# The order of loads and work in a fused attention and FFN block on one core: FFN weights moved in the sync engine's queue

## The chip, the cores and the metric

The kernel runs on one core of a Trainium2 chip. The time is the device time of one execution in microseconds (us), the median of several runs. One further execution was profiled; its own time and its span, from the first to the last instruction, are given below. The engines are named as in the profile: PE (TensorE, matmuls) with its weight loads PEld, DVE (VectorE), ACT (ScalarE), POOL (GpSimd) and SP (SyncE, which here issues every DMA transfer).

## What is computed

A transformer block for 2048 tokens of width 512, all in bf16: a layernorm, linear attention with 32 heads of 16, a residual, a layernorm, an FFN of width 1792 with a ReLU, and a residual.

```python
def _A_ref(x, wqkv, wo):
    B, S, D = x.shape
    H = 32; Dh = D // H
    qkv = (lambda x, *d: x.transpose(*d))((x @ wqkv).reshape(B, S, 3, H, Dh), 2, 0, 3, 1, 4)
    q, k, v = qkv[0], qkv[1], qkv[2]
    phi = lambda t: jnp.where(t > 0, t + 1, jnp.exp(t)) + 1e-6
    pq, pk = phi(q), phi(k)
    kv = jnp.einsum("bhsd,bhse->bhde", pk, v)
    z = jnp.einsum("bhsd->bhd", pk)
    num = jnp.einsum("bhqd,bhde->bhqe", pq, kv)
    den = jnp.einsum("bhqd,bhd->bhq", pq, z)[..., None] + 1e-6
    o = num / den
    return (lambda x, *d: x.transpose(*d))(o, 0, 2, 1, 3).reshape(B, S, D) @ wo
...
h = x + _A_ref(_layernorm(x, axis=-1), A_wqkv, A_wo)
h2 = h + _B_ref(_layernorm(h, axis=-1), B_w1, B_w2)   # relu(x @ w1) @ w2
```

## The kernel before

The order of all work is written out by hand. The string `ORDER` holds 567 words; each word names a small function `op_...` and its numbers, and a loop at the end calls them one after the other. There is no scheduler behind it: each engine runs its instructions in the order of the words that fall to it, and each instruction waits on semaphores for what it reads and overwrites. So an order has five queues in it, and an instruction that waits holds up everything behind it on its engine. A DMA transfer's place in SP's queue is the place of its word.

The 2048 tokens are 16 tiles of 128 rows (the numbers 0 to 15 behind most words) and four blocks of 512 tokens (0 to 3). The words, by stage:

- Loads, by SP: `lx.t.n` loads n tiles of x; `lk`, `lq`, `lv`, `lo` load the weights of k, q, v and the output projection (`lv` and `lo` in halves of 256 KB), `l1.0.2` and `l1.2.2` the two halves of w1 and `l2.0.7` and `l2.7.7` those of w2, 896 KB each. All but `lx` go through the helper `load_d` (L216).
- First layernorm: `S` and `A` (statistics, DVE), `R` (rstd, ACT), `N` (normalize, DVE). The normalized tile is turned with PE (`T`, and `E` on ACT copies it out) for tiles 0 to 4, and by a DMA transpose `X` (L290, SP) for the others.
- `K.t.b` (L298) and `Q.c.j.b` (L306) are the projections into PSUM bank b; `F`, `U`, `M`, `D` and `qF`, `qU`, `qM`, `qD` make phi of them (exp and relu on ACT, min and add on DVE). `G.t` (L350) accumulates the product of the normalized x and phi(k) in banks 4 to 7. `za`, `zf`, `zhi`, `zlo`, `z`, `zc`, `zh` sum phi(k) over the tokens; `gA`, `gD`, `kv`, `kx`, `m`, `mA`, `mD` make the state times the projections of v and of the output, `m_sb`.
- The denominators, block by block: `d4.c` (L422, PE), `dl4.c` and `dx4.c` (ACT, logarithm and exponential) give the reciprocals. They have to stand on 16 partitions each, so `wb.c` (L450) stores them to a DRAM scratch and eight transfers `rb.c.0` to `rb.c.7` (L453, 64 KB each) read them back, each repeated over 16 partitions, into `rr`. `rr` is one buffer for all four blocks. `dm.c.jb.2` (L466, DVE, two for each block) multiplies phi(q) by `rr` into `pqs`.
- `h.t.b` (L475, PE) multiplies `pqs` with `m_sb`, and `hD.t` (L481, DVE) adds x. Second layernorm: `s`, `a` (DVE), `r` (ACT), `n` (DVE) or `nA` (ACT, L258), then a PE transpose `t` with `v` (DVE) or `e` (ACT), or a DMA transpose `x` (L291, SP).
- FFN: `p.c.f.b` (L490) and `ph` (half of the tokens, L499), with ReLU by `pA` (ACT, L505) or `pD` (DVE, L510); `f.t.b.f0.n` (L519) is the second product, seven matmuls a word, `fo` (L527, DVE) scales and adds h, `fd` (L534, SP) stores.

The middle of SP's queue before reads, in order: ten `X` from `X.6`, `lv.2.2 lv.0.2 lo.0.2 lo.2.2 wb.0 l1.0.2`, the eight rows `rb.0`, `l1.2.2 l2.0.7 wb.1 x.1 x.0 rb.1.2 l2.7.7`, the other seven rows `rb.1`, `wb.2`, the eight rows `rb.2`, `wb.3 x.7` and the eight rows `rb.3`. Transfers of one queue are spread over 16 DMA engines; one is complete when all sixteen shares have landed.

Of the kernel before, what the change touches and what calls it, by code (L numbers as in the profile page):

```python
# [15 lines left out]


ORDER = """
table const masks warm.70.7.64 warm.2.7 lx.0.1 S.0 A.0 R.0.1 lx.1.1 lx.2.2 S.1 N.0.0.2 T.0.4.0.2 A.1 lk.0.4 S.2
N.0.2.2 lx.4.2 A.2 R.1.1 N.1 S.3 T.0.0.2.2 A.3 E.0.0.2 R.2.1 lx.6.2 E.0.2.2 T.1.3 E.1 N.2 R.3.1 lq.0.4 K.0.1.0.2  # L20
K.0.1.2.2 S.5 T.2.2 N.3 K.1.6.0.2 S.4 F.0.1 K.1.6.2.2 T.3.5 E.2 A.5 M.0.1 lx.8.4 K.2.4.0.2 K.2.4.2.2 U.0.1 E.3
A.4 S.6 S.7 R.4.2 A.6 N.4 Q.0.0.3 K.3.7.0.2 A.7 F.1.1 U.2.1 lx.12.4 N.5 R.6.2 F.2.1 M.1.1 S.11 X.5 U.1.1 N.6
D.0.1 D.1.1 X.6 T.4.5 Q.0.3.1 K.3.7.2.2 A.11 E.4 M.2.1 N.7 S.9 D.2.1 X.7 F.3.1 A.9 Q.0.1.4 S.12 M.3.1 U.3.1
qU.0.0.2 qF.0.0.2 K.4.5 K.5.6 A.12 S.10 S.8 S.13 U.4.2 F.4.2 A.10 A.8 Q.0.2.0 A.13 qM.0.0.2 D.3.1 R.8.2 N.8
K.6.2 M.4.2 R.10.2 K.7.3 G.1 S.14 N.9 A.14 R.12.2 D.4.2 X.8 G.2 G.3 G.0 G.5 N.13 qF.0.2.2 X.9 U.6.2 F.6.2 S.15
qM.0.2.2 A.15 X.13 R.14.2 qU.0.2.2 N.12 K.8.2 K.9.3 qD.0.0.2 M.6.2 N.11 N.14 N.10 X.12 X.11 D.6.2 qD.0.2.2 X.10
X.14 F.8.2 G.4 K.13.1 U.8.2 za.4.1 K.12.0 M.8.2 G.7 K.11.3 K.10.2 G.6 N.15 F.12.2 D.8.2 za.6.0 U.12.2 M.12.2
K.14.0 za.8.0 X.15 F.10.2 U.10.2 M.10.2 K.15.1 zf D.10.2 zhi D.12.2 lv.2.2 F.14.2 M.14.2 G.9 G.8 zlo lv.0.2 G.10
Q.1.1.3 lo.0.2 U.14.2 D.14.2 z.2.2 z.3.2 z.1.2 z.0.2 zc zh G.14 d4.0.0 dl4.0 dx4.0 G.12 G.15 G.13 G.11 Q.1.0.2
lo.2.2 gA.0.2 qF.1.0.2 Q.1.2.0 gD.2.2 kv.1.5 kv.3.5 kv.0.5 kv.2.5 Q.1.3.1 qU.1.0.2 Q.2.0.4 qM.1.0.2 qF.1.2.2 kx  # L30
m.1.3 m.0.2 m.2.6 qU.1.2.2 m.3.7 Q.2.1.5 wb.0 l1.0.2 rb.0.4 rb.0.3 rb.0.7 mA.2.2 rb.0.5 rb.0.1 qU.2.0.2 qD.1.0.2
Q.2.2.0 Q.2.3.1 qM.1.2.2 mD.0.2 rb.0.2 rb.0.0 rb.0.6 qF.2.0.2 dm.0.0.2 dm.0.2.2 l1.2.2 h.1.6 qU.2.2.2 qD.1.2.2
d4.1.2 hD.1 s.1 a.1 h.0.4 hD.0 s.0 l2.0.7 dl4.1 dx4.1 a.0 n.0 Q.3.0.3 h.3.7 Q.3.1.4 hD.3 nA.1 qF.2.2.2 wb.1 s.3
h.2.1 a.3 x.1 Q.3.3.6 qU.3.0.2 hD.2 n.3 s.2 Q.3.2.5 a.2 t.3.7 n.2 qM.2.2.2 qF.3.0.2 x.0 ph.0.0.2.0 v.3
ph.0.2.0.0 t.2.4 qU.3.2.2 v.2 ph.0.3.1.0 qM.2.0.2 qM.3.0.2 ph.0.1.3.0 r.0.4 qF.3.2.2 ph.0.1.3.1 ph.0.0.2.1
ph.0.3.1.1 qM.3.2.2 qD.2.2.2 pA.0.0.2 p.0.9.5 p.0.8.4 pA.0.8.2 ph.0.2.0.1 qD.3.2.2 qD.2.0.2 qD.3.0.2 d4.2.2.2
rb.1.2 l2.7.7 rb.1.1 rb.1.3 rb.1.0 rb.1.7 p.0.6.6 p.0.7.7 rb.1.4 rb.1.5 rb.1.6 dm.1.2.2 dm.1.0.2 pD.0.2.2 dl4.2
h.7.5 dl4.3 dx4.2 wb.2 h.5.3 rb.2.4 pD.0.6.2 hD.7 h.6.0 hD.5 s.7 hD.6 a.7 s.5 s.6 p.0.5.6 p.0.4.5 a.5 rb.2.3
rb.2.5 pD.0.4.2 rb.2.6 a.6 p.0.12.1 h.4.3 p.0.11.7 hD.4 p.0.10.6 p.0.13.2 n.6 dx4.3 s.4 rb.2.0 rb.2.7 rb.2.1
rb.2.2 f.1.0.0.7 n.7 a.4 n.5 n.4 dm.2.0.2 dm.2.2.2 pD.0.12.2 pD.0.10.2 h.11.3 h.9.5 wb.3 x.7 rb.3.0 rb.3.6 h.8.2  # L40
h.10.1 r.4.4 hD.11 hD.9 s.11 hD.8 rb.3.3 rb.3.2 a.11 hD.10 s.9 f.1.0.7.7 rb.3.5 rb.3.7 rb.3.1 rb.3.4 s.8
dm.3.0.2 dm.3.2.2 s.10 f.3.4.0.7 f.2.7.0.7 a.9 a.8 h.12.6 a.10 fo.1 hD.12 h.13.1 h.14.3 n.9 n.11 s.12 hD.14
r.8.4 h.15.6 x.4 x.6 x.5 f.2.7.7.7 a.12 hD.13 hD.15 s.14 s.15 s.13 a.14 a.15 a.13 n.14 n.8 n.10 n.12 n.13 fo.2
fd.1 x.11 x.9 p.1.11.3 p.1.10.2 p.1.6.0 p.1.7.1 p.1.9.6 p.1.8.5 n.15 f.3.4.7.7 f.0.7.0.7 pA.1.6.2 pA.1.10.2
pD.1.8.2 x.10 fo.3 f.0.7.7.7 p.1.1.5 p.1.0.4 fo.0 p.1.5.1 p.1.4.0 r.12.4 x.8 p.1.12.2 p.1.3.7 fd.3 pA.1.0.2 x.13
fd.0 p.1.2.6 p.1.13.3 pA.1.4.2 pD.1.2.2 pA.1.12.2 p.2.10.0 p.2.11.1 pA.2.10.2 x.15 x.14 p.2.9.4 p.2.8.3 p.2.4.6
p.2.5.7 p.2.3.2 x.12 fd.2 p.2.2.1 pD.2.8.2 p.2.6.4 pA.2.4.2 p.2.7.5 pA.2.2.2 pD.2.6.2 p.2.13.2 p.2.12.1
pA.2.12.2 f.4.6.0.7 f.4.6.7.7 f.5.7.0.7 fo.4 f.5.7.7.7 fo.5 f.7.3.0.7 p.2.0.6 p.2.1.7 pA.2.0.2 f.7.3.7.7 fo.7
p.3.0.4 p.3.1.5 f.6.1.0.7 p.3.2.2 pD.3.0.2 p.3.3.3 pA.3.2.2 f.6.1.7.7 fo.6 p.3.7.7 p.3.6.6 p.3.13.3 p.3.12.2
pA.3.6.2 fd.5 p.3.9.5 pD.3.12.2 p.3.8.4 pA.3.8.2 p.3.10.1 p.3.11.2 pA.3.10.2 p.3.4.6 p.3.5.7 pD.3.4.2 f.8.2.0.7  # L50
fd.7 f.15.5.0.14.0.2 fo.15.0.2 fd.4 f.8.2.7.7 fo.8 f.9.3.0.7 f.9.3.7.7 fd.6 f.13.5.0.7 fd.15.0.2 f.13.5.7.7
f.11.1.0.7 fo.9 fd.9 f.11.1.7.7 fo.13 fo.11 fd.8 f.12.4.0.7 f.12.4.7.7 fo.12 fd.13 fd.11 fd.12 f.14.2.0.7
f.14.2.7.7 fo.14 fd.14 f.10.6.0.7 f.10.6.7.7 fo.10 fd.10 f.15.0.0.14.3.1 fo.15.3.1 fd.15.3.1 f.15.1.0.14.2.1
fo.15.2.1 fd.15.2.1
"""


# [1 line left out]
def kernel(  # L59
# [155 lines left out]
    def load_d(dst, src, k, n):
        nc.sync.dma_start(out=dst[:, k : k + n, :], in_=src[:, k : k + n, :])  # L216
# [353 lines left out]
```

## Time and profile before

| | us |
|---|---|
| median of 3 runs (lowest, highest) | 170.49 (169.94, 170.64) |
| the profiled execution | 170.41 |
| its span | 168.7 |
| PE busy | 163.0 (97%) |
| DVE busy | 98.4 (58%) |
| ACT busy | 64.1 (38%) |
| granted TensorE clock | 1.00 |

The profiled execution is one run: its time is the span and what lies around it. Engines and DMA over the span, in 40 slices of 4.2 us (tenths):

```profile
PE   7799999999999997999999999999999999999993
...
DVE  3999999932689958999999511212204122213213
ACT  3799976815898763010011422442020242000000
...
DMA  5974155714896591413621335000011000011111
```

The slices show PE full from the third to the last but one, apart from the sixteenth (63 to 67 us); DVE full from 4 to 34 us and for most of 42 to 88; ACT mostly idle from 67 us on; DMA busiest at 4 to 8, 42 to 51 and 59 to 63 us. Times in the text are microseconds from the span's start.

### The profile page before, as it was taken

How to read it: one execution, taken by the hardware profiler on the slowest of the kernel's cores; microseconds unless marked ns; L12 is line 12 of the kernel's file. 1: busy time of each engine (PE TensorE's matmuls, PEld its weight loads, DVE VectorE, ACT ScalarE, POOL GpSimd, SP SyncE). 2: the span in 40 equal slices, each digit the busy share in tenths (PEclk: the TensorE clock that was granted, in tenths of full speed). 3: DMA queues.
4: the chain of work that ended last, by engine and by line, in shares of the span. 5: the costliest groups of instructions: out<-in, count | busy, mean ns of one | idle time of the engine just before them, and what ended most of it. 6: DMA issues, size and time to landing. Idle time of an engine off the chain costs nothing.

```text
span 168.7 us, 2429 instructions
## 1 busy us (share of the span) xinstructions
PE 163.0 (97%) x924; PEld 79.3 (47%) x924; DVE 98.4 (58%) x204; ACT 64.1 (38%) x98; POOL 4.9 (3%) x21
## 2 busy tenths in 40 slices
PE   7799999999999997999999999999999999999993
...
DVE  3999999932689958999999511212204122213213
ACT  3799976815898763010011422442020242000000
...
DMA  5974155714896591413621335000011000011111
GB/s 125 343 284 91 33 104 108 219 40 145 224 323 185 169 204 40 148 25 111 119 63 32 61 100 122 0 0 0 0 35 62 10 21 0 16 60 38 49 44 47
DMA packets 24859, 16.01 MB, mean 95 GB/s; under 512 B 14992, under 2 KB 23696, under 8 KB 24848
## 3 DMA queue, kind: packets, MB, share of 16 engines
...
q8 instruction: 7, 0.11, 0.3%
...
## 4 chain that ended last, share of the span: by engine, by line
PE 85%; DVE 6%; DMA 4%; SPq 2%; issue 1%; ACT 0%; DVEq 0%
PE bk L519 29%; PE bk L490 25%; PE bk L298 8%; PE bk L350 8%; PE bk L475 7%; PE bk L306 6%; DMA rr<-scr 3%; SPq L453 2%; DVE st L232 1%; DMA x_nat<-in_A_x_dram 1%; DVE h_nat L481 1%; DVE st L230 1%; DVE pqs L466 1%; PE bk L374 1%; PE bk L396 1%
## 5 line engine op out<-in xcount | busy, mean ns | idle before, releaser
L519 PE MATMUL bk<-w_sb,at 128*128 128x512 bf16 (+2 forms) x252 | 49.9, 355 | 0.0
L490 PE MATMUL bk<-lnT,w_sb 128*128 128x512 bf16 x208 | 46.7, 379 | 0.0
L519 PEld LDWEIGHTS <-at 128*128 128x128 bf16 x252 | 23.6, 98 | 25.2
L505 ACT ACTIVATE at<-bk 128x1024 bf16<-128x1024 f32 x16 | 16.3, 1024 | 43.2 <-PE bk L490 41.3
L490 PEld LDWEIGHTS <-w_sb 128*128 128x128 bf16 x208 | 20.3, 98 | 24.7 <-issue 0.7
L527 DVE SCALAR_TENSOR_TENSOR gT<-bk,rstd,h_nat 128x512 bf16<-128x512 f32 (+2 forms) x18 | 12.4, 689 | 32.4 <-PE bk L519 32.3
L510 DVE TENSOR_SCALAR at<-bk 128x1024 bf16<-128x1024 f32 x12 | 14.5, 1218 | 21.5 <-PE bk L490 20.1
L316 ACT ACTIVATE eb<-bk 128x1024 bf16<-128x1024 f32 (+1 forms) x18 | 16.8, 933 | 3.8 <-PE bk L298 2.7
L319 ACT ACTIVATE rb<-bk 128x1024 bf16<-128x1024 f32 (+1 forms) x18 | 16.7, 935 | 1.2 <-PE bk L306 1.2
L475 PE MATMUL bk<-m_sb,pqs 128*128 128x512 bf16 x64 | 15.1, 379 | 1.1 <-DVE pqs L466 1.1
L298 PE MATMUL bk<-wk_sb,lnT 128*128 128x512 bf16 x64 | 15.6, 379 | 0.1
L306 PE MATMUL bk<-lnT,wq_sb 128*128 128x512 bf16 x64 | 15.6, 379 | 0.0
L350 PE MATMUL bk<-at,h_nat 128*128 128x512 bf16 x56 | 13.4, 379 | 0.0
L236 ACT ACTIVATE rstd<-mv,eps 128x2 f32<-128x2 f32 (+2 forms) x14 | 4.2, 299 | 21.9 <-DVE mv L233 19.3
L230 DVE BATCH_NORM_STATS2 st<-x_nat 128x6 f32<-128x512 bf16 x16 | 10.6, 676 | 1.7 <-DMA x_nat<-in_A_x_dram 1.7
L481 DVE TENSOR_TENSOR h_nat<-bk,x_nat 128x512 bf16<-128x512 f32 x16 | 10.5, 672 | 0.5 <-PE bk L475 0.5
L232 DVE BATCH_NORM_STATS2 st<-h_nat 128x6 f32<-128x512 bf16 x16 | 10.6, 680 | 0.1
L475 PEld LDWEIGHTS <-pqs 128*128 128x128 bf16 x64 | 6.1, 98 | 8.9 <-DVE pqs L466 1.8
L306 PEld LDWEIGHTS <-wq_sb 128*128 128x128 bf16 x64 | 6.2, 98 | 7.2 <-DMA wq_sb<-in_A_wqkv_dram 0.3
L350 PEld LDWEIGHTS <-h_nat 128*128 128x128 bf16 x64 | 6.1, 98 | 7.3 <-issue 0.2
L298 PEld LDWEIGHTS <-lnT 128*128 128x128 bf16 x64 | 6.1, 98 | 7.1 <-issue 0.2
L323 DVE TENSOR_SCALAR eb<-eb 128x1024 bf16<-128x1024 bf16 (+1 forms) x18 | 6.8, 385 | 1.4 <-ACT eb L316 1.3
...
## 6 DMA issues: line engine op xcount, KB each, us to landing
...
```

Source lines behind the costliest of these rows:

```text
L230: op_S = lambda t: nc.vector.bn_stats(out=st[:, t, :], in_=x_nat[:, t, :])
L298: nc.tensor.matmul(bk[:, b, :], lhsT=lnT[c][:, kd, j * P : (j + 1) * P], rhs=wk_sb[:, kd, :], start=(kd == 0), stop=(kd == KD - 1),)
L306: nc.tensor.matmul(bk[:, b, :], lhsT=wq_sb[:, kd, j * P : (j + 1) * P], rhs=lnT[c][:, kd, :], start=(kd == 0), stop=(kd == KD - 1),)
L316: nc.scalar.activation(out=buf(eb, kind, i, n), in_=bank(at_bank[kind, i], n), func=ACT.Exp)
L319: nc.scalar.activation(out=buf(rb, kind, i, n), in_=bank(at_bank[kind, i], n), func=ACT.Relu)
L350: nc.tensor.matmul(bk[:, KD + kd, :], lhsT=ln_nat[:, t, kd * P : (kd + 1) * P], rhs=pk(t)[:, 0, :], start=(not stated), stop=(len(stated) ...
L475: nc.tensor.matmul(bk[:, b, :], lhsT=pqs[:, (c * KD + jb) % NQ, j * P : (j + 1) * P], rhs=m_sb[:, jb, :], start=(jb == 0), stop=(jb == KD ...
L490: nc.tensor.matmul(bk[:, b, :], lhsT=w1_sb[:, kd, f * P : (f + 1) * P], rhs=lnT[c][:, kd, :], start=(kd == 0), stop=(kd == KD - 1),)
L505: nc.scalar.activation(out=acts[c % 2][:, f : f + n, :], in_=bank(at_bank["p", c, f], n), func=ACT.Relu, scale=-1.0)
L510: nc.vector.tensor_scalar(out=acts[c % 2][:, f : f + n, :], in0=bank(at_bank["p", c, f], n), scalar1=-1.0, scalar2=0.0, op0=ALU.mult, op1= ...
L519: nc.tensor.matmul(bk[:, b, 0 : w * P], lhsT=acts[c % 2][:, f, j * P : (j + 1) * P], rhs=w2_sb[:, f, k * P : (k + w) * P], start=(f == 0), ...
L527: nc.vector.scalar_tensor_tensor(out=o_t[:, t % NO, cols], in0=bk[:, at_bank["f", t, k], 0 : w * P], scalar=rstd2[:, t : t + 1], in1=h_nat ...
```

## The change

The string `ORDER` is replaced by another order of 567 words, with the same loads, projections, blocks and products. In SP's queue `lv.2.2` goes behind `lx.12.4` and ahead of `X.5`, and `lo.2.2` behind `X.7`; `l2.0.7` and `l1.0.2` stand ahead of `wb.0`, `l1.2.2` behind the eight rows of block 0, then come `x.1 x.0 wb.1` and the eight rows of block 1, `wb.2 rb.2.4 rb.2.5 rb.2.0 l2.7.7 rb.2.1 rb.2.6 rb.2.7 wb.3 rb.2.2 rb.2.3`, and the rows of block 3 with `x.5` and `x.6` among them. On PE the order is the same up to `T.3` but for bank numbers; further on single words change places: `d4.2` stands behind four `p` in place of two, `h.6` opens block 1 in place of `h.7`, two words of `f` stand ahead of block 2's `h` in place of one, `h.14` comes behind the `p` of blocks 1 and 2, and those are mixed. Seven `n` become `nA`, two `pD` become `pA` (18 in place of 16), one `v` an `e`. A function `op_ax`, which would load x through ACT's queue, is added; no word calls it. The core of the diff:

```diff
 ORDER = """
...
-A.4 S.6 S.7 R.4.2 A.6 N.4 Q.0.0.3 K.3.7.0.2 A.7 F.1.1 U.2.1 lx.12.4 N.5 R.6.2 F.2.1 M.1.1 S.11 X.5 U.1.1 N.6
-D.0.1 D.1.1 X.6 T.4.5 Q.0.3.1 K.3.7.2.2 A.11 E.4 M.2.1 N.7 S.9 D.2.1 X.7 F.3.1 A.9 Q.0.1.4 S.12 M.3.1 U.3.1
...
-K.14.0 za.8.0 X.15 F.10.2 U.10.2 M.10.2 K.15.1 zf D.10.2 zhi D.12.2 lv.2.2 F.14.2 M.14.2 G.9 G.8 zlo lv.0.2 G.10
-Q.1.1.3 lo.0.2 U.14.2 D.14.2 z.2.2 z.3.2 z.1.2 z.0.2 zc zh G.14 d4.0.0 dl4.0 dx4.0 G.12 G.15 G.13 G.11 Q.1.0.2
-lo.2.2 gA.0.2 qF.1.0.2 Q.1.2.0 gD.2.2 kv.1.5 kv.3.5 kv.0.5 kv.2.5 Q.1.3.1 qU.1.0.2 Q.2.0.4 qM.1.0.2 qF.1.2.2 kx
-m.1.3 m.0.2 m.2.6 qU.1.2.2 m.3.7 Q.2.1.5 wb.0 l1.0.2 rb.0.4 rb.0.3 rb.0.7 mA.2.2 rb.0.5 rb.0.1 qU.2.0.2 qD.1.0.2
-Q.2.2.0 Q.2.3.1 qM.1.2.2 mD.0.2 rb.0.2 rb.0.0 rb.0.6 qF.2.0.2 dm.0.0.2 dm.0.2.2 l1.2.2 h.1.6 qU.2.2.2 qD.1.2.2
-d4.1.2 hD.1 s.1 a.1 h.0.4 hD.0 s.0 l2.0.7 dl4.1 dx4.1 a.0 n.0 Q.3.0.3 h.3.7 Q.3.1.4 hD.3 nA.1 qF.2.2.2 wb.1 s.3
-h.2.1 a.3 x.1 Q.3.3.6 qU.3.0.2 hD.2 n.3 s.2 Q.3.2.5 a.2 t.3.7 n.2 qM.2.2.2 qF.3.0.2 x.0 ph.0.0.2.0 v.3
-ph.0.2.0.0 t.2.4 qU.3.2.2 v.2 ph.0.3.1.0 qM.2.0.2 qM.3.0.2 ph.0.1.3.0 r.0.4 qF.3.2.2 ph.0.1.3.1 ph.0.0.2.1
-ph.0.3.1.1 qM.3.2.2 qD.2.2.2 pA.0.0.2 p.0.9.5 p.0.8.4 pA.0.8.2 ph.0.2.0.1 qD.3.2.2 qD.2.0.2 qD.3.0.2 d4.2.2.2
-rb.1.2 l2.7.7 rb.1.1 rb.1.3 rb.1.0 rb.1.7 p.0.6.6 p.0.7.7 rb.1.4 rb.1.5 rb.1.6 dm.1.2.2 dm.1.0.2 pD.0.2.2 dl4.2
-h.7.5 dl4.3 dx4.2 wb.2 h.5.3 rb.2.4 pD.0.6.2 hD.7 h.6.0 hD.5 s.7 hD.6 a.7 s.5 s.6 p.0.5.6 p.0.4.5 a.5 rb.2.3
-rb.2.5 pD.0.4.2 rb.2.6 a.6 p.0.12.1 h.4.3 p.0.11.7 hD.4 p.0.10.6 p.0.13.2 n.6 dx4.3 s.4 rb.2.0 rb.2.7 rb.2.1
-rb.2.2 f.1.0.0.7 n.7 a.4 n.5 n.4 dm.2.0.2 dm.2.2.2 pD.0.12.2 pD.0.10.2 h.11.3 h.9.5 wb.3 x.7 rb.3.0 rb.3.6 h.8.2
-h.10.1 r.4.4 hD.11 hD.9 s.11 hD.8 rb.3.3 rb.3.2 a.11 hD.10 s.9 f.1.0.7.7 rb.3.5 rb.3.7 rb.3.1 rb.3.4 s.8
-dm.3.0.2 dm.3.2.2 s.10 f.3.4.0.7 f.2.7.0.7 a.9 a.8 h.12.6 a.10 fo.1 hD.12 h.13.1 h.14.3 n.9 n.11 s.12 hD.14
...
...
+T.2.7 S.5 lq.0.4 R.3.1 K.1.6.0.2 K.1.6.2.2 N.3 E.2 T.3.5 U.0.1 S.4 K.2.3.0.2 S.7 A.4 lx.8.4 E.3 A.5 F.0.1 A.7
+S.6 R.4.2 M.0.1 A.6 lx.12.4 N.5 N.4 F.1.1 K.2.3.2.2 lv.2.2 R.6.2 Q.0.3.1 K.3.0.0.2 U.1.1 F.2.1 Q.0.1.5 T.4.2 E.4
+D.0.1 K.3.0.2.2 Q.0.0.4 F.3.1 N.6 S.10 M.1.1 N.7 D.1.1 S.9 M.2.1 U.3.1 K.4.6 U.2.1 X.5 K.5.7 S.12 S.13 S.8 X.6
...
+M.12.2 za.8.0 K.14.0 D.12.2 X.15 F.10.2 K.15.1 M.10.2 U.10.2 zf lo.0.2 D.10.2 G.9 G.8 zhi G.10 Q.1.1.3 F.14.2
+M.14.2 zlo U.14.2 D.14.2 z.3.2 z.2.2 z.1.2 z.0.2 G.14 zc zh d4.0.2 dl4.0 G.12 dx4.0 G.15 G.13 G.11 Q.1.0.2
+gA.2.2 lv.0.2 l2.0.7 l1.0.2 qU.1.0.2 Q.1.2.0 gD.0.2 wb.0 kv.3.7 kv.1.7 kv.0.7 kv.2.7 qF.1.0.2 kx qM.1.0.2
+Q.1.3.1 Q.2.0.4 qD.1.0.2 m.1.3 qU.1.2.2 rb.0.5 m.3.7 m.0.2 qF.1.2.2 m.2.6 Q.2.1.5 Q.2.3.1 rb.0.0 rb.0.2 mA.2.2
+rb.0.7 mD.0.2 rb.0.3 qF.2.0.2 qU.2.0.2 rb.0.4 rb.0.6 rb.0.1 Q.2.2.0 dm.0.2.2 dm.0.0.2 qM.1.2.2 h.1.2 qD.1.2.2
+qF.2.2.2 h.0.3 d4.1.4 hD.1 s.1 a.1 hD.0 nA.1 dl4.1 dx4.1 qU.2.2.2 h.2.5 h.3.7 Q.3.1.3 Q.3.0.2 qF.3.0.2 l1.2.2
+s.0 a.0 n.0 hD.3 x.1 x.0 Q.3.3.7 s.3 wb.1 rb.1.1 rb.1.3 qU.3.0.2 a.3 hD.2 rb.1.5 n.3 Q.3.2.6 t.3.4 e.3
+ph.0.2.0.0 ph.0.0.2.0 s.2 a.2 n.2 t.2.5 qF.3.2.2 ph.0.3.1.0 ph.0.1.3.0 v.2 ph.0.2.0.1 ph.0.0.2.1 rb.1.7
+ph.0.1.3.1 ph.0.3.1.1 qM.3.2.2 qU.3.2.2 p.0.8.5 p.0.9.6 pA.0.0.2 rb.1.4 qD.3.2.2 qM.3.0.2 qM.2.0.2 pA.0.2.2
+qD.2.0.2 rb.1.0 pA.0.8.2 p.0.13.3 p.0.7.7 qM.2.2.2 qD.2.2.2 qD.3.0.2 rb.1.2 d4.2.5.2 dl4.2 dx4.2 dl4.3 rb.1.6
+dm.1.0.2 dm.1.2.2 h.6.0 hD.6 h.5.2 dx4.3 r.0.4 h.7.5 hD.7 hD.5 p.0.10.0 s.5 wb.2 a.5 p.0.11.1 p.0.4.4 p.0.6.6
+p.0.5.5 rb.2.4 rb.2.5 s.7 nA.5 pA.0.6.2 pA.0.10.2 s.6 rb.2.0 l2.7.7 rb.2.1 rb.2.6 rb.2.7 p.0.12.2 pD.0.4.2 h.4.7
+hD.4 s.4 wb.3 rb.2.2 f.2.4.0.7 f.0.0.0.7 rb.2.3 dm.2.0.2 dm.2.2.2 a.4 h.10.1 pA.0.12.2 h.8.5 hD.10 a.6 nA.4
+h.11.3 a.7 hD.8 s.8 rb.3.1 f.3.7.0.7 rb.3.3 h.9.1 rb.3.5 x.5 f.2.4.7.7 s.10 fo.2 f.0.0.7.7 f.1.4.0.7 rb.3.6
+rb.3.2 rb.3.0 rb.3.7 nA.6 x.6 rb.3.4 hD.11 hD.9 a.10 fo.0 a.8 nA.7 f.3.7.7.7 s.9 x.4 x.7 f.1.4.7.7 n.10 n.8 a.9
+fo.3 dm.3.0.2 p.1.9.5 p.1.5.7 s.11 a.11 nA.11 p.1.10.1 nA.9 fo.1 dm.3.2.2 h.12.3 h.15.0 hD.15 hD.12 s.15 a.15
+p.1.4.6 p.1.8.4 p.1.11.2 pA.1.4.2 x.10 h.13.6 p.1.0.3 s.12 pD.1.8.2 p.1.1.4 hD.13 a.12 r.8.4 fd.0 n.12 pA.1.0.2
...
-    loads = [w.split(".") for w in ORDER.split() if w.startswith("lx.")]
+    loads = [w.split(".") for w in ORDER.split() if w[:3] in ("lx.", "ax.")]
...
+    def op_ax(t, n):
+        nc.scalar.dma_start(out=x_nat[:, t : t + n, :], in_=rows_of(xf, t, n))
```

More of the change, by code (lines that the diff above doesn't have):

```diff
@@ L18 @@
 ORDER = """
-table const masks warm.70.7.64 warm.2.7 lx.0.1 S.0 A.0 R.0.1 lx.1.1 lx.2.2 S.1 N.0.0.2 T.0.4.0.2 A.1 lk.0.4 S.2
-N.0.2.2 lx.4.2 A.2 R.1.1 N.1 S.3 T.0.0.2.2 A.3 E.0.0.2 R.2.1 lx.6.2 E.0.2.2 T.1.3 E.1 N.2 R.3.1 lq.0.4 K.0.1.0.2
-K.0.1.2.2 S.5 T.2.2 N.3 K.1.6.0.2 S.4 F.0.1 K.1.6.2.2 T.3.5 E.2 A.5 M.0.1 lx.8.4 K.2.4.0.2 K.2.4.2.2 U.0.1 E.3
-A.4 S.6 S.7 R.4.2 A.6 N.4 Q.0.0.3 K.3.7.0.2 A.7 F.1.1 U.2.1 lx.12.4 N.5 R.6.2 F.2.1 M.1.1 S.11 X.5 U.1.1 N.6
-D.0.1 D.1.1 X.6 T.4.5 Q.0.3.1 K.3.7.2.2 A.11 E.4 M.2.1 N.7 S.9 D.2.1 X.7 F.3.1 A.9 Q.0.1.4 S.12 M.3.1 U.3.1
@@ L24 @@
[L24 to L27, printed above, removed]
-K.14.0 za.8.0 X.15 F.10.2 U.10.2 M.10.2 K.15.1 zf D.10.2 zhi D.12.2 lv.2.2 F.14.2 M.14.2 G.9 G.8 zlo lv.0.2 G.10
@@ L39 @@
-rb.2.5 pD.0.4.2 rb.2.6 a.6 p.0.12.1 h.4.3 p.0.11.7 hD.4 p.0.10.6 p.0.13.2 n.6 dx4.3 s.4 rb.2.0 rb.2.7 rb.2.1
-rb.2.2 f.1.0.0.7 n.7 a.4 n.5 n.4 dm.2.0.2 dm.2.2.2 pD.0.12.2 pD.0.10.2 h.11.3 h.9.5 wb.3 x.7 rb.3.0 rb.3.6 h.8.2
-h.10.1 r.4.4 hD.11 hD.9 s.11 hD.8 rb.3.3 rb.3.2 a.11 hD.10 s.9 f.1.0.7.7 rb.3.5 rb.3.7 rb.3.1 rb.3.4 s.8
-dm.3.0.2 dm.3.2.2 s.10 f.3.4.0.7 f.2.7.0.7 a.9 a.8 h.12.6 a.10 fo.1 hD.12 h.13.1 h.14.3 n.9 n.11 s.12 hD.14
-r.8.4 h.15.6 x.4 x.6 x.5 f.2.7.7.7 a.12 hD.13 hD.15 s.14 s.15 s.13 a.14 a.15 a.13 n.14 n.8 n.10 n.12 n.13 fo.2
@@ L44 @@
[L44 to L53, printed above, removed]
@@ L54 @@
-fo.15.2.1 fd.15.2.1
+table const masks warm.70.7.64 warm.2.7 lx.0.1 S.0 A.0 R.0.1 lx.1.1 S.1 N.0.0.2 A.1 R.1.1 lx.2.2 S.2 T.0.5.0.2
+E.0.0.2 N.0.2.2 lk.0.4 A.2 N.1 lx.4.2 lx.6.2 S.3 T.0.6.2.2 R.2.1 N.2 T.1.1 K.0.2.0.2 E.0.2.2 E.1 K.0.2.2.2 A.3
+T.2.7 S.5 lq.0.4 R.3.1 K.1.6.0.2 K.1.6.2.2 N.3 E.2 T.3.5 U.0.1 S.4 K.2.3.0.2 S.7 A.4 lx.8.4 E.3 A.5 F.0.1 A.7
+S.6 R.4.2 M.0.1 A.6 lx.12.4 N.5 N.4 F.1.1 K.2.3.2.2 lv.2.2 R.6.2 Q.0.3.1 K.3.0.0.2 U.1.1 F.2.1 Q.0.1.5 T.4.2 E.4
+D.0.1 K.3.0.2.2 Q.0.0.4 F.3.1 N.6 S.10 M.1.1 N.7 D.1.1 S.9 M.2.1 U.3.1 K.4.6 U.2.1 X.5 K.5.7 S.12 S.13 S.8 X.6
```

14 lines of the change are left out of this document (added).

## The prediction

> **What bounds the kernel now.** I read the page first (TensorE, PE, is busy for 97% of the span), then the waits of PE, then the chain around the one place where PE stands still, then the SP queue's timeline, which issues every transfer.
>
> Waits of PE (engine and line, what it waited for, us, times, longest), and PE's timeline at the place:
> ```profile
> PE bk L475 <- DVE pqs L466: 1.1, 1, 1.1
> PE bk L227 <- DVE m_sb L185: 1.1, 1, 1.1
> PE bk L269 <- DVE h_nat L244: 0.6, 1, 0.6
> ...
> 65.39 2.76 PE L475 MATMUL bk<-m_sb,pqs 128*128 128x512 bf16 x12 [1.06 <-DVE pqs L466]
> ```
> From the first `K` (6.71) to the last matmul (near 166) PE has one idle gap: 1.06 us ahead of `h.7`, the first `h` of block 1. The other two are ahead of 6 us. Every matmul of the change is there before it too, so PE's work is the same sum, and the end moves only by what PE waits.
>
> The chain of waits into that gap (start, us, what):
> ```profile
> 55.68 0.42 SPq L216
> 56.15 0.55 SPq L453
> ...
> 59.09 4.83 DMA rr<-scr
> ...
> 64.04 1.30 DVE pqs L466 x2
> 65.35 0.05 issue
> 65.39 0.82 PE bk L475 x3
> ```
> L216 is `l2.7.7`, the second half of w2 (896 KB), issued behind one row of block 1's reciprocals and ahead of seven. Its own landing, and those of the rows (L453) in two stretches, 51 to 61 and 66 to 71 us:
> ```profile
> DMA to landing us min/median/max: 6.6/6.6/6.6
> ...
> DMA to landing us min/median/max: 2.7/5.5/6.4
> ...
> DMA to landing us min/median/max: 2.2/2.5/2.6
> ```
> With `l2.7.7` among them rows take up to 6.4 us, alone (block 2) 2.5. By the trace's landing marks `l2.7.7` is complete at 62.24, the first row behind it at 62.58, the last at 63.93; `dm.1` (L466) starts at 64.04, 1.30 us for two, and `h.7` follows. What DMA moved meanwhile (stretch, then busy time of the engines, clock, DMA share, GB/s):
> ```profile
> 58.00:60.00 2.00, 2.00 (x19) 1.66 (x17) 2.00 (x6) 1.20 (x2) 0.00 (x0) 1.00 0.99 353
> 60.00:62.00 2.00, 2.00 (x16) 1.00 (x17) 1.55 (x3) 0.86 (x2) 0.00 (x0) 1.00 1.18 195
> 62.00:64.00 2.00, 2.00 (x16) 0.71 (x10) 0.00 (x0) 2.00 (x4) 0.00 (x0) 1.00 0.24 50
> ```
> The engines were full for four microseconds; a row sits in their queues behind the weights.
>
> **The change, part by part.**
>
> *Loads ahead of `wb.0`, and none among the rows of block 1.* `l2.0.7` and `l1.0.2` now stand behind `lv.0.2`, ahead of the store `wb.0`; `l1.2.2` follows block 0's eight rows. SP was free from 31.2 to 38.9 and DMA nearly so, and 1.8 MB at the 340 to 374 GB/s of 50 to 52 us takes some 5 us, so they are in before `wb.0`. Block 0's rows come about 1 us sooner, which buys nothing: `h.1` stands at the same sum of PE work (48.70), and `dm.0` now follows `mD`, which waits for `m.0` as third of the four `m`. `mD` 46.1 to 47.3 and `dm.0` to 48.6 leave 0.1 us; 0, give or take 0.1.
>
> For block 1 SP issues `x.1`, `x.0`, then `wb.1`. `x.0` ended its issue at about 55.0 before (SP's timeline: two transposes from 52.25, 2.76 us), and neither its input nor `x.1`'s moves, so `wb.1` goes at 55.0; the first row follows a store by 1.78 us (64.28 to 66.06): 56.8. An undisturbed set of rows takes 5.77 us from its first issue to its last landing (66.06 to 71.83): 62.6. `dm.1` takes 1.3 us, and `h.6` can start on its first half at 63.4. PE gets there at 64.33, where it stopped before. The gap is gone: **-1.06 us**, with 0.9 us in hand.
>
> *Where the stall goes.* `l2.7.7` is still among rows, now block 2's: `wb.2 rb.2.4 rb.2.5 rb.2.0 l2.7.7 rb.2.1 rb.2.6 rb.2.7 wb.3 rb.2.2 rb.2.3`. The words of the change say none between; the order says otherwise. Block 2 is also later: `d4.2` moves behind `p.0.13` and `p.0.7`, from 61.89 to 63.62 (two `p`, 1.73 us). `wb.0` was issued 1.83 us after `d4.0` began (37.10 to 38.93), so `wb.2` at 65.45, its first row at 67.23, `l2.7.7` 1.37 us on (three issues of block 2) at 68.60. Block 1 is the pattern: from the issue of `l2.7.7` to the last landing of the seven rows behind it took 8.25 us (55.68 to 63.93). Now five rows and a store of 128 KB stand behind, the same 448 KB. So 76.85. Half of the sixteen shares of that last row had landed by 63.1, 0.83 us sooner; if none lags, 76.0. Against that, the page's instruction queue q8 moves a 16 KB packet of 1.1 us at 73.6, in the middle of the new window (an earlier one, at 52.2, held one share of a store back by 1.25 us): up to 77.9 if it meets a lagging share. I take 76.9, the row's own figure.
>
> PE reaches `h.10`, the first `h` of block 2, later than it reached `h.11`: 75.72 less the 1.06, plus seven more `f` matmuls (1.51): 76.17. `dm.2` starts 0.11 after landing; `h.10` needs its first half (0.65 and 0.04 to hand over) and, 0.43 into its four matmuls, the second half, 0.2 late: 1.0 in all. So it can run as from 77.9: **+1.75 us**, with ends 0.85 (76.0) and 2.75 (77.9). Behind the wait are all of PE's queue and, as `rr` is one buffer, the eight rows of block 3, with two transposes among them: 5.77 + 2 x 1.3 us after `dm.2`, near 87, while their `dm.3` stands behind `fo.3`, near 89.
>
> The Trainium skill, "DMA: Bandwidth & Descriptors", section "Queues, rings and completion order", says that each DMA engine takes the descriptors of a queue in order, and that a completion mark lands only after every earlier write of that engine. This speaks against the change: no row behind `l2.7.7` may complete ahead of it, however small. Block 1's row marks agree (62.58 behind 62.24). By it the term is +1.75; if rows could pass, the last would land 2.5 us after its issue near 71.5, at 74.0, and the term would be 0.
>
> *The head.* `lv.2.2` (256 KB) now stands behind `lx.12.4`, ahead of the first transpose `X.5`. The last share of `lx.12.4` landed at 13.52 and `X.5` at 14.03; the two halves of wv landed 0.66 apart, so `X.5` lands between 14.03 and 14.69. `K.5` reaches it at 14.42: 0 to 0.3, I take **+0.1**. Up to the first `K` PE and ACT keep their order; a change there is within 0.1.
>
> *Engines.* Seven `n` go to ACT as `nA`, two `pD` become `pA`, one `v` an `e`. DVE loses 7 x 0.34 + 2 x 1.22 + 0.42 = 5.2 us, ACT gains 7 x 0.72 + 2 x 1.02 + 0.60 = 7.7. On ACT it is hidden by idle time (the `rstd` of L236 waited 9.56 and 9.69 us in 64 to 85, the `pA` of L505 41.3 us in all). Without that cover the `x` of block 1 would be late; they have over 1 us until `p.1.9`. 0. The bank numbers, the blocks of `p.1`, `p.2` mixed and `h.14` put back to 113: where I followed the banks their last readers end 0.3 us or more ahead; 0. `ax` is defined and used by no word.
>
> Sum: -1.06 + 1.75 + 0.1 = **+0.8 us**. The profiled execution took 170.41 us (span 168.7), 0.08 under the median of 170.49; so 170.41 + 0.8 = **171.2 us**.
>
> **The rivals.** *Rows of block 2 in time.* `l2.7.7` may drain faster: with `l1.2.2` and `l2.0.7` together 340 to 419 GB/s stood for 4 us from 48, with no lagging share. It decides if the last row of block 2 is in by 75.2; then only the gap is removed: 170.41 - 1.06 = 169.35, faster. For it: half of block 1's shares were early. Against: the same bytes behind, the same tiny rows (195 GB/s from 60 to 62). *A smaller stall*, 0.2 to 0.9 us, landing at 75.4 to 76.1: 169.6 to 170.5, taken as 170.2. *A larger one*: the fetch at 73.6 falls on a lagging share, or the store `wb.3` holds the two rows behind it longer than two rows would; landing from 77.9 on, stall 2.75: 172.2. *The gap at block 1 stays*: `wb.1` now stands behind both transposes (first row 56.8 in place of 55.10), and if the rows take more than 6.7 us, 0.9 over block 2's, PE waits there again; with all 1.06 back, 172.3. Against: nothing else is in the queues there.
>
> **How the numbers follow.** Forecast 0.50 (170.7 to 171.9), rows in time 0.17, smaller stall 0.13, larger 0.12, gap stays 0.08. About 0.5%, 0.85 us, is what a measurement of this kernel can tell from no change: under 169.64 is faster, over 171.34 slower. Faster: the first rival without the runs that lose at the head, 0.15. Same: the 0.02 of it left, 0.13, and half the forecast, 0.26: 0.41. Slower: 0.24 + 0.12 + 0.08 = 0.44. The range takes in the first rival and most of the large stall: 169.4 to 172.4; the forecast's own is 170.7 to 171.9.
>
> **What would show it.** Right: no PE idle ahead of `h.6` near 64.3, PE idle of 0.8 to 2.7 us ahead of `h.10` near 76.2, put down to DVE `pqs`, with DVE before it waiting for `rr<-scr`; rows of block 2 with up to 6 us to landing, those of block 1 near 2.5. Wrong: PE idle at another place, such as an `h` of block 0, a `p` waiting for a bank, or no idle at all between 7 and 166 us.

## The result, and the profile after

The changed kernel takes 171.03 us (median of 20 runs, 170.49 to 171.99) against 170.44 us for the kernel before (20 runs, 169.85 to 171.47): a ratio of 1.0038, interval 1.0022 to 1.0054. Of the kernel's median that is 0.65 us (0.0038 x 170.44). The interval lies clear of 1, so the changed kernel is a little slower; but the difference is less than the 0.85 us (0.5 per cent) that the prediction took as the least it could tell, so by its own bounds (169.64 to 171.34) the two kernels are the same. The profiled execution took 171.7 us with a span of 170.0, so it is one of the longer ones; a second profile of the same kernel, the shortest of its twelve runs (170.72 us, span 169.0), is drawn on below. Two runs further on, one of E3 (171.46 us) and one of the kernel before beside E5 to E8 (172.41 us), took over 1.5 per cent more than the fastest of their kernel, a slower state of the machine, and count in no ratio.

Three lines of the page of the changed kernel: the span in 40 slices of 4.25 us, busy tenths.
```profile
PE   7899999999999999996999999999999999999993
...
DVE  3899999942489884765497490354700550211233
...
DMA  5997354683361330480473420000330220000012
```
The dip of PE has moved from the sixteenth slice (63 to 67 us) to the nineteenth (76 to 81). DMA has its own hump just before it, in the eighteenth. DVE is free for half of the nineteenth slice, so it is hardly short of time there, although it is the engine that the next view names.

Waits of PE in the changed kernel (engine and line, what it waited for, us, times, longest):
```profile
PE bk L478 <- DVE pqs L469: 1.4, 1, 1.4
PE bk L230 <- DVE m_sb L185: 1.1, 1, 1.1
PE bk L272 <- DVE h_nat L247: 0.5, 1, 0.5
```
Line numbers from the loads on are 3 higher than in the kernel before: L478 is `h`, L469 `dm`, L456 the rows `rb`, L453 the store `wb`, L219 the weight loads. There is again one idle gap of note, of 1.4 in place of 1.1, with the same names. Where it stands only the timeline tells.

Timeline of PE around it (start, us, line, what, instructions, idle before):
```profile
65.13 2.76 PE L478 MATMUL bk<-m_sb,pqs 128*128 128x512 bf16 x12
67.73 5.34 PE L493 MATMUL bk<-lnT,w_sb 128*128 128x512 bf16 x24
72.91 1.03 PE L478 MATMUL bk<-m_sb,pqs 128*128 128x512 bf16 x4
73.77 3.19 PE L522 MATMUL bk<-w_sb,at 128*128 128x512 bf16 x14
78.38 2.93 PE L478 MATMUL bk<-m_sb,pqs 128*128 128x512 bf16 x12 [1.42 <-DVE pqs L469]
```
The first line is `h.6`, which opens block 1: no idle time ahead of it. The last is `h.10`, the first of block 2: 1.42 us idle, and its three words take 2.93 us where twelve matmuls without a wait take 2.75, since the second half of `dm.2` comes a little late.

The chain of waits into that gap (start, us, what):
```profile
69.50 0.42 SPq L219
69.97 0.56 SPq L456
...
71.91 0.34 SPq L453
...
72.31 0.42 SPq L456
...
72.78 4.76 DMA rr<-scr
...
77.63 0.70 DVE pqs L469
78.33 0.05 issue
78.38 0.99 PE bk L478 x3
```
L219 at 69.50 is `l2.7.7`. Everything that SP issues behind it, five rows and the store `wb.3`, is in the queues by 73.2, and then the chain stands still for 4.76 us in the last row. `dm.2` itself is done in 0.70 us a half. DVE's timeline has what it waited for (in brackets, us and releaser):
```profile
77.63 1.29 DVE L469 TENSOR_TENSOR pqs<-pqT,rr 128x1024 bf16<-128x1024 bf16 x2 [2.16 <-DMA rr<-scr]
```
It stood idle for 2.16 us until the rows were in: DVE is only the messenger.

From issue to landing in the changed kernel: `l2.7.7`, the eight rows of block 2, and those of block 1.
```profile
DMA to landing us min/median/max: 6.0/6.0/6.0
...
DMA to landing us min/median/max: 2.4/4.9/5.8
...
DMA to landing us min/median/max: 2.7/2.9/3.1
```
Block 1's rows, now without a load among them, need 3.1 us at most where they needed up to 6.4; block 2's now need up to 5.8 where they needed 2.6.

### The profile page after: what moved, and what is told of

Same layout as the page of the kernel before. It is cut to its first block, busy times and chain, and to the rows that moved or that the text cites. A ratio compares the mean times of both kernels' runs of the same rounds, so it can differ in the third digit from the quotient of the medians.

```text
span 170.0 us, 2428 instructions
## 1 busy us (share of the span) xinstructions
PE 164.0 (96%) x924; PEld 79.6 (47%) x924; DVE 95.4 (56%) x194; ACT 71.3 (42%) x108; POOL 4.7 (3%) x21
## 4 chain that ended last, share of the span: by engine, by line
PE 78%; DMA 11%; SPq 5%; ACT 2%; DVE 1%; issue 1%; DVEq 0%
PE bk L522 27%; PE bk L493 23%; PE bk L301 7%; PE bk L478 6%; PE bk L353 6%; PE bk L309 5%; DMA rr<-scr 4%; DMA wq_sb<-in_A_wqkv_dram 4%; SPq L456 3%; DMA scr<-rd 2%; PE bk L502 2%; SPq L213 1%; DVE pqs L469 1%; ACT ld L431 1%; ACT rd L436 1%
## 5 line engine op out<-in xcount | busy, mean ns | idle before, releaser
L522 PE MATMUL bk<-w_sb,at 128*128 128x512 bf16 (+2 forms) x252 | 49.4, 355 | 0.0
L493 PE MATMUL bk<-lnT,w_sb 128*128 128x512 bf16 x208 | 46.2, 379 | 0.0
L508 ACT ACTIVATE at<-bk 128x1024 bf16<-128x1024 f32 x18 | 17.8, 1022 | 41.4 <-PE bk L493 40.5
L513 DVE TENSOR_SCALAR at<-bk 128x1024 bf16<-128x1024 f32 x10 | 12.2, 1215 | 14.3 <-PE bk L493 14.3
L478 PE MATMUL bk<-m_sb,pqs 128*128 128x512 bf16 x64 | 15.5, 380 | 1.5 <-DVE pqs L469 1.4
L261 ACT ACTIVATE hn<-h_nat,mv 128x512 bf16<-128x512 bf16 x8 | 5.6, 717 | 22.4 <-DVE mv L236 22.4
L478 PEld LDWEIGHTS <-pqs 128*128 128x128 bf16 x64 | 5.9, 98 | 10.0 <-DVE pqs L469 3.4
```

The costliest lines, as they stand in the source:

```text
L478: nc.tensor.matmul(bk[:, b, :], lhsT=pqs[:, (c * KD + jb) % NQ, j * P : (j + 1) * P], rhs=m_sb[:, jb, :], start=(jb == 0), stop=(jb == KD ...
L493: nc.tensor.matmul(bk[:, b, :], lhsT=w1_sb[:, kd, f * P : (f + 1) * P], rhs=lnT[c][:, kd, :], start=(kd == 0), stop=(kd == KD - 1),)
L508: nc.scalar.activation(out=acts[c % 2][:, f : f + n, :], in_=bank(at_bank["p", c, f], n), func=ACT.Relu, scale=-1.0)
L513: nc.vector.tensor_scalar(out=acts[c % 2][:, f : f + n, :], in0=bank(at_bank["p", c, f], n), scalar1=-1.0, scalar2=0.0, op0=ALU.mult, op1= ...
L522: nc.tensor.matmul(bk[:, b, 0 : w * P], lhsT=acts[c % 2][:, f, j * P : (j + 1) * P], rhs=w2_sb[:, f, k * P : (k + w) * P], start=(f == 0), ...
```

## The experiments

Each kernel was timed in five rounds beside the kernel before on the same chip. E1 to E4 share one set of runs of it (median 170.61 us), E5 to E8 another (170.38). In E1 to E3 and E6 to E8 the lines are 1 lower than in the changed kernel (L477 is `h`, L300 is `K`); in E4, which is made from the kernel before, `h` is L474. Only words of `ORDER` are moved; the diffs show them with their neighbours. A profile shows one execution of several, and these scatter by up to 2 us: the profiles of E3, E5 and E8 are of the shortest or second shortest run of their kernel, those of E4 and E6 of the longest.

**E1: the second half of w2 ahead of block 1's store.**

```diff
-qF.3.0.2 l1.2.2 s.0
+qF.3.0.2 l1.2.2 l2.7.7 s.0
...
-rb.2.0 l2.7.7 rb.2.1
+rb.2.0 rb.2.1
```

> The changed order with one word moved: l2.7.7 from among the rows of block 2 to behind l1.2.2, ahead of x.1. Theory (the weights among the rows make the stall): the rows of block 2 land in about 2.5 us each, the last near 74 where it was 77.5; no PE idle ahead of h.10; 1.4 us less than the changed kernel, so a median of about 169.6 against 170.44 before, a ratio near 0.995. Rival A (block 2 is late by itself, since d4.2 stands behind two more p): PE idle ahead of h.10 stays at 1 us or more and the time is as for the changed kernel, ratio 1.004. Rival B (the weights only move their harm: wb.1 or x.1 now wait behind them): the gap comes back ahead of h.6, 0.5 to 1 us, ratio near 1.000.

169.03 us, ratio 0.9918 (0.9901 to 0.9936). Rows of block 2 in E1, then PE's timeline at block 2:
```profile
DMA to landing us min/median/max: 2.3/2.6/2.6
...
72.87 3.18 PE L521 MATMUL bk<-w_sb,at 128*128 128x512 bf16 x14
75.89 2.75 PE L477 MATMUL bk<-m_sb,pqs 128*128 128x512 bf16 x12
```
With one load out of block 2's rows the gap ahead of `h.10` is gone, and no other gap of PE is listed after 7 us. `d4.2` and the store `wb.3` stand where the change put them, so neither of them makes the gap. `x.1` and `x.0`, now behind the load, cost nothing that shows. Against the changed kernel's 1.0038, from another set of runs, this one word is worth 1.2 per cent, some 2.0 us, rather more than the 1.77 us that the gap is worth in the first profile (by the starts of the matmuls around it, as worked out below).

**E2: the same load behind the last row of block 2.**

```diff
-rb.2.0 l2.7.7 rb.2.1
+rb.2.0 rb.2.1
...
-rb.2.3 dm.2.0.2
+rb.2.3 l2.7.7 dm.2.0.2
```

> The changed order with l2.7.7 moved behind the last row of block 2. Theory: the gap ahead of h.10 is gone, as in the run before it; the second half of w2 lands near 79 to 80, in time for f.2.4.7.7 near 80; the rows of block 3 come later by up to 3 us but are covered; ratio near 0.995. Rival A (block 2 late by itself): gap of 1 us or more, ratio 1.004. Rival C (the weights come too late for f.2.4.7.7): PE waits there for w_sb, 0.5 to 2 us, ratio 0.998 to 1.007.

169.42 us, ratio 0.9933 (0.9909 to 0.9958). Two waits of PE in E2, after those before 7 us:
```profile
PE bk L477 <- DVE pqs L468: 0.4, 1, 0.4
PE bk L300 <- DMA lnT<-h_nat: 0.3, 1, 0.3
```
The first is not at `h.10` (which starts at 76.73 with no idle time) but at `h.1`, at 49.67; the second is at `K.5`. So placing the load behind the rows cures the stall as well as placing it early: by the landing marks it is complete at 78.90, and the first product that reads it starts at 81.69 without a wait. What was not expected is that `h.1` and `K.5` cost something here; E6 to E8 go after that.

**E3: seven matmuls more ahead of `h.10`, the load left where it is.**

```diff
-f.0.0.0.7 rb.2.3
+f.0.0.0.7 f.3.7.0.7 rb.2.3
...
-rb.3.1 f.3.7.0.7 rb.3.3
+rb.3.1 rb.3.3
```

> The changed order with f.3.7.0.7, seven matmuls or 1.51 us, moved ahead of h.10, and every transfer left where it is. Theory (the stall is the lateness of the rows against PE's place in its order): the rows land as late as before, 77.5, but PE gets to h.10 1.51 us later and waits 0 to 0.1 us; 1.3 to 1.4 us less, ratio near 0.995. Rival (the stall has another source, such as DVE's queue behind dm.2 or a bank): it moves on to the next h or f and the time stays, ratio 1.004.

169.71 us, the median of the eleven runs that the ratio is taken from; ratio 0.9947 (0.9923 to 0.9971), with a wide scatter (168.9 to 170.89). Rows of block 2 in E3, then PE's timeline:
```profile
DMA to landing us min/median/max: 2.4/4.8/6.0
...
72.64 4.70 PE L521 MATMUL bk<-w_sb,at 128*128 128x512 bf16 x21
77.17 3.77 PE L477 MATMUL bk<-m_sb,pqs 128*128 128x512 bf16 x16
```
The rows are as late as in the changed kernel, but PE has 21 matmuls in place of 14 to do and comes to `h.10` at 77.17. The stall is a matter of who arrives first, not of the rows as such: in this execution 1.51 us of other work hides nearly all of it. It is the second shortest of the twelve (168.97 us), so what the longer ones lose is not seen here.

**E4: the kernel before, with only `l2.7.7` moved behind block 1's rows.**

```diff
-rb.1.2 l2.7.7 rb.1.1
+rb.1.2 rb.1.1
...
-rb.1.6 dm.1.2.2
+rb.1.6 l2.7.7 dm.1.2.2
```

> The order before with one word moved: l2.7.7 from behind the first row of block 1 to behind its last row. Theory (the same cause made the gap ahead of h.7): the rows of block 1 land by about 61, no PE idle ahead of h.7, 1.06 us less than before, ratio near 0.994, unless the rows of block 2 now wait behind the weights: these have 6 us until they are needed. Rival (the gap ahead of h.7 comes from the store wb.1, late behind l2.0.7, or from the rows' own pace): the gap stays at 0.5 us or more, ratio 0.997 to 1.000.

169.21 us, ratio 0.9919 (0.9901 to 0.9936). PE's timeline in E4 at block 1, the landing of block 1's rows, and the one wait of PE after 7 us:
```profile
63.30 1.90 PE L489 MATMUL bk<-lnT,w_sb 128*128 128x512 bf16 x8
65.04 2.75 PE L474 MATMUL bk<-m_sb,pqs 128*128 128x512 bf16 x12
...
DMA to landing us min/median/max: 2.5/2.6/2.8
...
PE bk L498 <- DMA lnT<-hn: 0.2, 1, 0.2
```
So the gap of the kernel before has the same cause as that of the changed one: the load among the rows. 0.0081 x 170.61 is 1.38 us; the gap was 1.22 us by the starts of the matmuls on its two sides. The whole of the old gap is had back by moving one word.

**E5: the changed kernel once more.**

> The changed kernel as it is, beside the three that follow, on one chip. Every theory: a ratio of 1.004 to the kernel before, one PE gap of 1.2 to 1.7 us ahead of h.10, waits of 0 to 0.3 us each at K.5 or K.7 (for the transposes X.5 and X.7) and at h.1 (for dm.0).

171.37 us, ratio 1.0053 (1.0025 to 1.0081). Its waits of PE, those before 7 us left out:
```profile
PE bk L478 <- DVE pqs L469: 1.2, 1, 1.2
...
PE bk L301 <- DMA lnT<-h_nat: 0.2, 1, 0.2
```
The slowdown holds on another set of runs, and so does the gap at `h.10`, with 0.2 us less. The wait at `K.5` shows here and not in the first profile: the head of the kernel varies from one execution to the next (the first `K` starts at 7.17 in the first profile and at 6.61 in this one).

**E6: the FFN loads where the kernel before had them, but `l2.7.7` behind block 1's rows.**

```diff
-lv.0.2 l2.0.7 l1.0.2 qU.1.0.2
+lv.0.2 qU.1.0.2
...
-wb.0 kv.3.7
+wb.0 l1.0.2 kv.3.7
...
-l1.2.2 s.0
+l1.2.2 l2.0.7 s.0
...
-rb.1.6 dm.1.0.2
+rb.1.6 l2.7.7 dm.1.0.2
...
-rb.2.0 l2.7.7 rb.2.1
+rb.2.0 rb.2.1
```

> The changed order with the FFN loads put where the order before had them, but none among rows: l1.0.2 behind wb.0, l1.2.2 and l2.0.7 behind block 0's rows, l2.7.7 behind block 1's. Theory (only the weights among the rows counted; the loads ahead of the first store bought nothing): no gap ahead of h.6 and h.10, the same time as with l2.7.7 early (ratio 0.992), give or take 0.002; rows of block 0 a microsecond later, h.1 at most 0.3 us late. Rival (the early loads are what freed block 1's rows): l2.0.7 now lands near 53 and holds x.1 or wb.1 back, PE idle ahead of h.6 of 0.5 us or more, ratio 0.995 or higher.

169.27 us, ratio 0.9926 (0.9902 to 0.9951). There is no gap at `h.6` or `h.10`; one wait of PE after 7 us:
```profile
PE bk L300 <- DMA lnT<-h_nat: 0.5, 1, 0.5
```
So loading `l2.0.7` and `l1.0.2` ahead of `wb.0`, the part of the change that its words put first, is worth nothing that can be seen: its interval and that of E1, which has them early, lie over each other. The wait at `K.5`, 0.5 us, was larger than expected.

**E7: `lv.2.2` and `lo.2.2` back behind the transposes, all else as changed.**

```diff
-K.2.3.2.2 lv.2.2 R.6.2
+K.2.3.2.2 R.6.2
...
-F.6.2 lo.2.2 A.10
+F.6.2 A.10
...
-X.15 F.10.2
+X.15 lv.2.2 lo.2.2 F.10.2
```

> The changed order with lv.2.2 and lo.2.2 put back behind X.15, nothing else. Theory: the waits at K.5 and K.7 go (0.1 to 0.3 us less), but 2.8 MB instead of 2.3 MB now stand between X.15 and wb.0; wb.0 lands near 43.5 where it was 42.2, dm.0 comes as late, and PE waits 0.8 to 1.5 us ahead of h.1; the gap ahead of h.10 stays. Sum: 0.5 to 1.2 us slower than the changed kernel, ratio 1.007 to 1.011. Rival (weights ahead of the store cost nothing, since the store is small): no wait ahead of h.1, ratio 1.002 to 1.004.

171.63 us, ratio 1.0071 (1.0052 to 1.0091). PE's timeline at `h.1` in E7, then its waits:
```profile
49.80 1.90 PE L477 MATMUL bk<-m_sb,pqs 128*128 128x512 bf16 x8 [0.73 <-DVE pqs L468]
...
PE bk L477 <- DVE pqs L468: 2.0, 2, 1.3
...
PE bk L308 <- DMA wq_sb<-in_A_wqkv_dram: 0.6, 1, 0.6
```
The wait at `K.5` is gone as expected, but no time is saved. The 0.5 MB of these two loads now stand in the queues ahead of the two FFN loads and of `wb.0`: the store takes 3.24 us to land in place of 2.50, and `h.1`, which had 0.23 us to wait, has 0.73 by this view (0.89 by the starts). The wait for `wq_sb` ahead of the first `Q` (0.6 us in this view, 0.72 by the starts) was not expected. It differs from one execution to the next: by the starts it is 0 to 0.19 us in eight of the other nine profiles and 0.31 in the first one of the changed kernel. The ratio is not apart from that of E5.

**E8: only one FFN load ahead of `wb.0`, and none among the rows of a block.**

```diff
-K.2.3.2.2 lv.2.2 R.6.2
+K.2.3.2.2 R.6.2
...
-F.6.2 lo.2.2 A.10
+F.6.2 A.10
...
-X.15 F.10.2
+X.15 lv.2.2 lo.2.2 F.10.2
...
-lv.0.2 l2.0.7 l1.0.2 qU.1.0.2
+lv.0.2 l1.0.2 qU.1.0.2
...
-l1.2.2 s.0
+l1.2.2 l2.0.7 s.0
...
-rb.1.6 dm.1.0.2
+rb.1.6 l2.7.7 dm.1.0.2
...
-rb.2.0 l2.7.7 rb.2.1
+rb.2.0 rb.2.1
```

> All of it put together: the changed order with lv.2.2 and lo.2.2 behind X.15, l1.0.2 alone ahead of wb.0, l1.2.2 and l2.0.7 behind block 0's rows, l2.7.7 behind block 1's. Theory: no wait at K.5, K.7, h.1, h.6 or h.10; the least of all, ratio 0.990 to 0.992. Rival (1.9 MB ahead of the store is as bad as 2.3): wait of 0.2 us or more ahead of h.1, ratio 0.992 to 0.995.

168.87 us, ratio 0.9903 (0.9867 to 0.9939): the lowest median of all, below both kernels, though its interval overlaps those of E1 and E4. PE's timeline in E8 at block 0 and at block 2:
```profile
45.85 2.75 PE L308 MATMUL bk<-lnT,wq_sb 128*128 128x512 bf16 x12
48.44 1.89 PE L477 MATMUL bk<-m_sb,pqs 128*128 128x512 bf16 x8
...
72.46 3.19 PE L521 MATMUL bk<-w_sb,at 128*128 128x512 bf16 x14
75.48 2.84 PE L477 MATMUL bk<-m_sb,pqs 128*128 128x512 bf16 x12
```
From the twelve `Q` matmuls to `h.1` it is 2.59 us, their bare time, and no wait of PE is listed after 7 us. `wb.0` lands 1.72 us after its issue, although `lv.2.2` and `lo.2.2` stand ahead of it as in E7; with the second FFN load there as well it was 3.24 (E7).

## Why the prediction was right, and where its terms were off

The forecast was 171.2 us, 0.8 over the execution that it started from; the median is 171.03. Its two large terms hold, and the experiments show their cause. Two small ones were mis-sized, and one was not in it. The terms as predicted, beside the two profiles of the changed kernel; here a wait is the distance between the starts of the matmuls on its two sides less their bare time, which for the old gap gives 1.22 us where the list of waits has 1.06 (that list goes by the ends of matmuls, which are modelled):

| step | predicted | first profile | second (E5) |
|---|---|---|---|
| gap ahead of `h.7`, block 1 | -1.06 | -1.22 | -1.22 |
| gap ahead of `h.10`, block 2, with the late second half (0.18) | +1.75 | +1.77 | +1.57 |
| `K.5` and `K.7` wait for their transposes | +0.1 | +0.18 | +0.34 |
| `h.1` waits for `dm.0` | 0 | +0.23 | 0 |
| small waits between `h.1` and block 2 in the kernel before | not in it | -0.26 | -0.27 |
| start of the first `K` | 0 | +0.46 | -0.10 |
| rest up to `h.1` | not in it | +0.17 | +0.03 |
| sum | +0.8 | +1.33 | +0.35 |

The sums agree with the spans, 170.0 and 169.0 against 168.7. The measured 0.65 us lies between them. The start of the first `K` is put down to the execution and not to the change: it is 7.17 in the first profile, where the third transfer of x landed at 5.52 us, and 6.34 to 6.73 in the nine others, where that landed at 4.59 to 4.79. Most of the 0.17 in the row below it is the longer wait for `wq_sb` in the first profile. That the total came out so near is in part luck: the 0.26 us of small waits that were not in the sum, and the 0.16 by which the old gap was taken too small, offset the 0.3 to 0.5 us that the stretch up to `h.1` cost beyond the 0.1 taken.

*The gap at block 1.* Right. `wb.1` went at 55.84 (predicted 55.0), its first row at 57.8 (56.8), the last landed at 63.82 (62.6): each about a microsecond late, as `h.1` was in that execution (49.74 for 48.70). With 0.8 us from the landing to a first half of `dm.1`, some 0.5 of the 0.9 us in hand was left when PE got there at 65.13. E4 shows that the load among the rows made the old gap: with the load behind them none is left.

*Where the stall went.* Right in place, kind and size. The order keeps `l2.7.7` among rows, three of block 2 ahead of it and five behind, whatever the words of the change say. E1 and E2 take it out in both directions and the gap goes; E3 covers it with PE work and it all but goes while the rows stay late. From the issue of `l2.7.7` to the last row behind it took 8.04 us in the first profile and 7.84 in E5's, for the 8.25 taken from block 1.

The size hides two errors that cancel, so that it came out so close is luck. The load landed faster than block 1's had (6.04 us in place of 6.56), which is what the first rival hoped for. What that had won was lost again on one of the 16 DMA engines: fifteen of the last row's sixteen shares had landed by 76.55, the last at 77.55. The jump is already there in the row before it, whose last share came at 77.37, 1.14 us after the whole of `wb.3` (76.23). The DMA view of the changed kernel from 73 to 77 us (kind: packets, MB, share of 16 engines) has two packets of instructions in that window:
```profile
q8 instruction: 1, 0.02, 1.7%
q14 instruction: 1, 0.01, 0.9%
```
1.7% of 16 engines over 4 us is 1.1 us on one engine, and that packet begins at 75.24; a fetch falling on a late share was the third rival's mechanism. In E8, where no load is near, a fetch that begins between 72 and 73 us goes with one share of the last row landing 1.15 us behind the other fifteen (3.6 us at most, median 2.6). In E3, E5 and E7, which have the load among the same rows and two such packets in the 3 us before, the last share lags by 0.5 to 0.7 us. That the fetch holds the share is read from these marks; no kernel was run that moves it, so it is not shown.

The prediction weighed a rule of the Trainium skill ("DMA: Bandwidth & Descriptors", section "Queues, rings and completion order"): a completion mark comes only after all earlier writes of that engine. This trace agrees: `rb.2.1` lands at 75.72, behind `l2.7.7` at 75.54, though it is 64 KB, and the store `wb.3` at 76.23 behind all rows ahead of it.

*The head.* Right in kind, mis-sized: 0.1 was taken, with 0.3 as the upper end. Over the six profiles that have `lv.2.2` and `lo.2.2` between the transposes the waits at `K.5` and `K.7` come to 0.18, 0.27, 0.50, 0, 0.34 and 0.63 us, 0.32 in the mean; with both back behind `X.15` (E7, E8) there is none. The step followed `lv.2.2` and `X.5` alone, by one execution's landing of x; that `X.7` is held up too (3.49 us to landing in the first profile, 2.82 and 2.97 in E7 and E8) was not priced.

*Loads ahead of `wb.0`.* The step said 1.8 MB take some 5 us from 31.2 and so are in before `wb.0`. That failed. They were issued at 31.3 and 31.8 and landed at 39.70 and 41.94; `wb.0`, issued at 39.74, stood in their tail, and block 0's rows did not come sooner (last landing 48.21, for 47.37 in the kernel before). What DMA moved (stretch; busy time and instructions of PE, PEld, DVE, ACT and POOL; clock; DMA share; GB/s), changed kernel:
```profile
31.00:33.00 2.00, 2.00 (x11) 0.94 (x10) 1.98 (x5) 2.00 (x3) 0.00 (x0) 1.00 0.69 206
33.00:35.00 2.00, 2.00 (x11) 0.92 (x10) 2.00 (x6) 1.75 (x2) 0.00 (x0) 1.00 0.73 232
35.00:37.00 2.00, 2.00 (x47) 1.43 (x45) 0.53 (x1) 0.00 (x0) 0.00 (x0) 1.00 0.90 310
37.00:39.00 2.00, 2.00 (x16) 0.76 (x14) 0.46 (x2) 0.63 (x1) 0.00 (x0) 1.00 0.91 354
```
The 340 to 374 GB/s of the step came from another stretch; here they were reached only at 37 us. The chain of the changed kernel from the store to `h.1` (start, us, what):
```profile
39.74 2.50 DMA scr<-rd
...
45.45 2.76 DMA rr<-scr
...
48.39 1.31 DVE pqs L469 x2
49.74 1.90 PE bk L478 x8
```
The store took 2.50 us for 1.75 in the kernel before, and `dm.0` started at 48.39 as its rows landed, not as `mD` let it. The 0.1 us in hand that the step had worked out was right, and so there was nothing to take the 0.75 us. Over the profiles of the changed order and of the runs made from it the wait at `h.1` goes with the time that `wb.0` takes to land: none for 1.72 to 1.97 us (E8, E1, E5), 0.09 and 0.23 for 2.33 and 2.50 (E3, changed), 0.54 and 0.89 for 2.85 and 3.24 (E2, E7). E6, with 0.21, has a load directly behind `wb.0`.

*Not in the sum.* The kernel before lost some 0.26 us in small waits between `h.1` and block 2 that the new order does not have. Without them the sum would have been 0.5.

*The rivals.* Rows of block 2 in time: no, they came 1.4 us late; but it is what E1, E2, E6 and E8 make true, and their 168.87 to 169.42 us lie within half a microsecond of the 169.35 worked out for it. A smaller stall and a larger one: no, though each had a part in the size. The gap at block 1 staying because `wb.1` stands behind the two transposes: no, in any kernel here.
